# Moving one softmax piece across a block boundary, and re-cutting its batch into pieces of 10, 6, 11 and 11 rows

## The chip, the cores and the metric

The kernel runs on one core of one Trainium2 chip. The metric is device time in microseconds of one execution. The profile is one execution recorded by the hardware profiler, and its span is some 1.7 us shorter than the time of the same run (734.8 us for 736.54).

In the profile's lines, PE is TensorE (matmuls), PEld its weight loads, DVE VectorE, ACT ScalarE, and L536 is line 536 of the kernel. Times in a timeline are microseconds from the span's start.

## The reference

A dynamic convolution, then a feed-forward network with a squared ReLU:

```
w   = softmax(weight_gen over the 7 taps)            # per token and head
out[b, s, h] = sum_k w[b, s, h, k] * x[b, s - 6 + k, h]   # 8 heads of 24 channels
h   = relu(out @ w_in)                                # 192 -> 2048
y   = (h * h) @ w_out                                 # 2048 -> 192
```

There are 8 batches of 4096 tokens. The matmuls of the feed-forward part fill PE; the softmax is side work for ScalarE (exponential) and VectorE (sum, reciprocal, scaling).

## The kernel before

The work is cut into blocks of 1024 tokens (the first two have 512). Each block has 16 units: 6 matmuls into `h`, a ReLU on ScalarE into `t1`, and a square on VectorE into `g`. The output matmuls `M` of block j - 1 are interleaved with the units of block j. A quarter of a block takes two `M` (units 0 to 7, then 8 to 15) of 32 matmuls each, into two banks of PSUM, the memory that the matmuls write. ScalarE then copies one bank into `o_sb`, and VectorE adds the other to it.

```
        nc.scalar.activation(out=t1[:, e], in_=h, func=ActF.Relu)
        n = 2 if PAIRED_FROM <= j and u < NF - 2 else 1    # units 14 and 15: single squares
        if e + 1 >= n:
            a = e + 1 - n
            nc.vector.tensor_tensor(                        # L536
                out=g[:, a : e + 1], in0=t1[:, a : e + 1], in1=t1[:, a : e + 1], op=AluOp.mult
            )
...
    ps_o = ctx.enter_context(tc.tile_pool(name="ps_o", bufs=1, space=...PSUM))   # o0, o1: one buffer each
...
        nc.scalar.copy(out=o_sb, in_=o[0][:, c])            # L574
        if len(o) == 2:
            nc.vector.tensor_tensor(out=o_sb, in0=o[1][:, c], in1=o_sb, op=AluOp.add)   # L576
```

A softmax of a whole batch covers 32 rows per partition and 6 of halo (rows that the next partition holds too). It is cut into four pieces, and each piece is placed at a point (block, unit) of the program: ahead of that unit, after the `M` that precedes it. A piece on VectorE is a sum, a reciprocal, and 4 scalings for each stretch of at most 8 rows that doesn't cross a multiple of 8. Its exponential on ScalarE has a place of its own, some units earlier.

```
        steady_spread = "MuMuuu" * 2 + "MuCMuuu" + "MuMuuu"    # u unit, M output matmuls, C convolution
...
        CUTS = {..., R: (0, 8, 18, 28, R + HALO)}              # default: 8, 10, 10, 10 rows
        CUTS_FOR = {(2, 1): (0, 11, R // 2 + HALO)}
        TIMES = {
            ...
            (3, 0): ((9, 9), (9, 13), (10, 9), (11, 9)),       # the fourth batch
        }
        def soft(s):
            lo, hi = next(s.softs)
            s.total(lo, hi)          # L257
            s.recip(lo, hi)          # L264
            s.scale(lo, hi, nc.vector)   # L272
```

The program orders all instructions by hand, and each engine takes its own in that order. The fourth batch is the first with this four-piece plan, and the only one of them with two pieces in one block: the later batches put one in each of four blocks.

The softmax here doesn't subtract the row's maximum and nothing guards it: scores larger than these inputs give would overflow.

## Time and profile before

| | before |
|---|---|
| time, first 3 runs | 736.59 us median (735.5 to 736.84) |
| profiled span | 734.8 us, clock 1.00 |
| block 9 to 10, first `M` after the convolution to the same place one block on | 23.28 us |
| its neighbours | 22.06, 22.08 us |
| PE idle recorded in that block | 23.28 - 22.60 = 0.68 us |

### The profile page before, as it was taken

The numbers are of one execution on the slowest core, as the hardware profiler recorded it, in microseconds if no ns is written. First come the engines' busy times: TensorE is split into PE (matmuls) and PEld (weight loads), VectorE is DVE, ScalarE is ACT, GpSimd is POOL, SyncE is SP. The second block draws the span as 40 slices with busy tenths as digits, with TensorE's granted clock in tenths as the row PEclk, the third lists the DMA queues.
The fourth block names the chain that finished last, engine by engine and source line by source line (L and its number), as shares of the span: only waits on it lengthen the run. The fifth ranks groups of instructions, "written<-read, shape, count | busy, mean of one in ns | idle before, by whom it ended". The sixth has DMA issues, their size and how long they took to land.

```text
span 734.8 us, 31124 instructions
## 1 busy us (share of the span) xinstructions
PE 725.9 (99%) x14106; PEld 529.4 (72%) x14106; DVE 627.3 (85%) x856; ACT 613.5 (83%) x724; POOL 100.2 (14%) x148
## 2 busy tenths in 40 slices
PE   7999999999999999999999999999999999999998
PEld 3767777777767777777777777777777777777777
DVE  5999898998899988889888889888889888778853
ACT  4998888988888888888888888888888888888883
POOL 7322222320001100011000110010100110001000
PEclk9999999999999999999999999999999999999999
DMA  7846444794444533454433554334544315444012
GB/s 210 130 81 138 80 62 104 144 165 120 92 74 99 122 76 73 66 137 100 80 65 76 116 124 85 59 64 127 103 87 83 61 48 121 66 87 78 29 45 66
DMA packets 126544, 68.71 MB, mean 93 GB/s; under 512 B 85193, under 2 KB 122636, under 8 KB 125900
## 3 DMA queue, kind: packets, MB, share of 16 engines
q1 hardware_dynamic: 80908, 48.12, 22.9%
q0 software_dynamic: 45360, 18.50, 21.6%
q8 instruction: 110, 1.80, 1.0%
q14 instruction: 22, 0.18, 0.1%
q10 hardware_dynamic: 144, 0.10, 0.0%
HBM read 50.18 MB, written 28.70 MB: 107 GB/s over the span
## 4 chain that ended last, share of the span: by engine, by line
PE 70%; DVE 0%; ACT 0%; issue 0%
PE o L560 35%; PE h L518 32%; PE yp L450 3%; DVE g L536 0%; ACT o_sb L574 0%
## 5 line engine op out<-in xcount | busy, mean ns | idle before, releaser
L532 ACT ACTIVATE t<-h 128x1024 f16<-128x1024 f32 x512 | 496.4, 1026 | 60.1 <-PE h L518 59.7
L560 PEld LDWEIGHTS <-g 64*128 64x128 f16 (+1 forms) x8032 | 342.8, 94 | 56.9 <-issue 2.5
L560 PE MATMUL o<-w_o,g 64*128 64x192 f16 (+1 forms) x8032 | 379.7, 243 | 0.7 <-DVE g L536 0.6
L536 DVE TENSOR_TENSOR g<-t 128x2048 f16<-128x2048 f16 (+1 forms) x309 | 309.2, 1037 | 27.6 <-ACT t L532 27.3
L518 PE MATMUL h<-y,w_p 64*128 64x512 f16 x2400 | 291.7, 376 | 0.0
L518 PEld LDWEIGHTS <-w_p 64*128 64x128 f16 x2400 | 113.8, 94 | 94.8
L381 DVE TENSOR_TENSOR bd<-wr,mask 128x4160 f16<-128x4160 f16 (+3 forms) x89 | 149.4, 1703 | 4.7 <-DMA wr<-v_first 4.7
L576 DVE TENSOR_TENSOR o_sb<-o,o_sb 128x384 f32<-128x384 f32 x123 | 68.4, 556 | 62.1 <-ACT o_sb L574 61.3
L333 POOL DMA_DIRECT2D xt<-in_x_dram x62 | 52.1, 844 | 422.6 <-PE yp L450 363.7
L574 ACT COPY o_sb<-o 128x384 f32<-128x384 f32 x129 | 61.5, 477 | 48.0 <-PE o L560 47.5
L518 PE MATMUL h<-y,w_i 64*128 64x512 f16 (+1 forms) x768 | 82.3, 350 | 1.8 <-ACT t L532 0.8
L518 PEld LDWEIGHTS <-w_i 64*128 64x128 f16 x768 | 37.2, 94 | 27.7 <-issue 4.0
L450 PEld LDWEIGHTS <-xt 128*32 128x32 f16 x2000 | 24.4, 95 | 10.6 <-issue 10.6
L272 DVE TENSOR_TENSOR v_big<-ex,rcp 128x112 f16<-128x112 f32 (+5 forms) x180 | 29.9, 237 | 2.1 <-DMA vd<-v_big 1.1
L460 DVE CAST y<-yp 128x1024 f16<-128x1024 f32 x25 | 30.4, 1218 | 0.0
L450 PE MATMUL yp<-bd,xt 128*32 128x104 f16 (+1 forms) x2000 | 28.3, 209 | 0.0
L250 ACT ACTIVATE ex<-wg 128x560 f32<-128x560 f32 (+4 forms) x38 | 25.9, 682 | 1.7 <-DMA wg<-in_weight_gen_dram 1.7
L257 DVE TENSOR_REDUCE ssum<-ex 128x80 f32<-128x560 f32 (+4 forms) x38 | 25.3, 666 | 2.2 <-ACT ex L250 2.2
L460 ACT CAST y<-yp 128x1024 f16<-128x1024 f32 x25 | 25.2, 1007 | 0.0
L264 DVE RECIPROCAL rcp<-ssum 128x80 f32<-128x80 f32 (+4 forms) x38 | 22.8, 600 | 1.3
L323 POOL DMA_DIRECT2D xt<-in_x_dram x7 | 3.9, 555 | 124.7 <-PE yp L450 109.7
L363 POOL DMA_DIRECT2D wr<-v_first x31 | 16.9, 565 | 15.9 <-DVE v_first L272 15.7
(34 smaller groups left out, 95.8 us busy)
## 6 DMA issues: line engine op xcount, KB each, us to landing
out_dram<-o_sb SPq DMA_DIRECT2D x63, 384.0 KB
xt<-in_x_dram POOLq DMA_DIRECT2D x42, 240.0 KB, 5.1
wg<-in_weight_gen_dram SPq DMA_DIRECT2D x4, 1064.0 KB
xt<-in_x_dram POOLq DMA_DIRECT2D x20, 192.0 KB, 4.6
wr<-vd SPq DMA_DIRECT2D x38, 80.0 KB
vd<-v_big SPq DMA_DIRECT2D x5, 512.0 KB
y<-y SPq DMA_DIRECT2D x100, 24.0 KB
wg<-in_weight_gen_dram SPq DMA_DIRECT2D x5, 392.0 KB
```

The lines of the kernel that those rows point to most:

```text
L250: nc.scalar.activation(out=self.ex[:, lo:hi].rearrange("p r g k e -> p (r g) k e"), in_=self.wg[:, lo:hi].rearrange("p r (g e) k -> p (r g ...
L272: eng.tensor_tensor(out=bass.AP(tensor=v.tensor, offset=v.offset + lo * H * SL + lo % SL * 2 + g * SL * 2, ap=[list(v.ap[0]), [H * SL + 2, ...
L333: eng.dma_start(out=dst[:, first:last], in_=ap)
L381: nc.vector.tensor_tensor(out=bd_t[j][:, H * lo : H * (lo + len(tiles) * n)].rearrange("p (g m c) -> p g m c", g=shape[1], c=2 * SL), in0= ...
L450: nc.tensor.matmul(out=yp[p0 : p0 + 32, k - k0, a:b], lhsT=x_t[s][:, i, c0 : c0 + 32], rhs=bd[:, head // 2, e, 0 : b - a], start=True, sto ...
L460: copy(out=y[:, k0 : k0 + 2], in_=yp)
L518: nc.tensor.matmul(out=h[:, half, jj * th : (jj + 1) * th], lhsT=w_in_chunk(w, u * per + jj, slot, half), rhs=y_t[j][r0 : r0 + RT, k, 0:th ...
L532: nc.scalar.activation(out=t1[:, e], in_=h, func=ActF.Relu)
L536: nc.vector.tensor_tensor(out=g[:, a : e + 1], in0=t1[:, a : e + 1], in1=t1[:, a : e + 1], op=AluOp.mult)
L560: nc.tensor.matmul(out=oo[:, cc * Dm : (cc + 1) * Dm], lhsT=g[r0 : r0 + n, cc * P : (cc + 1) * P], rhs=w_o[r0 : r0 + n, fc, :], start=(fc ...
L574: nc.scalar.copy(out=o_sb, in_=o[0][:, c])
L576: nc.vector.tensor_tensor(out=o_sb, in0=o[1][:, c], in1=o_sb, op=AluOp.add)
```

## The change

The intent is to take the second piece out of the way of block 9's last squares and put it where VectorE waits anyway, at the start of block 10, and to make it small enough for that hole. The other pieces take over its rows.

```diff
-        CUTS_FOR = {(2, 1): (0, 11, R // 2 + HALO)}
+        CUTS_FOR = {(2, 1): (0, 11, R // 2 + HALO), (3, 0): (0, 10, 16, 27, R + HALO)}
...
-            (3, 0): ((9, 9), (9, 13), (10, 9), (11, 9)),
+            (3, 0): ((9, 9), (10, 0), (10, 9), (11, 9)),
```

The second piece's exponential stays at the same unit, with 6 rows in place of 10.

## The prediction

> **What bounds the kernel now.** I read the page's busy shares first, then the chain that ended last, then each block by stretches of time, then the instructions in the stretch that stood out.
>
> ```profile
> PE 725.9 (99%) x14106; PEld 529.4 (72%) x14106; DVE 627.3 (85%) x856; ACT 613.5 (83%) x724; POOL 100.2 (14%) x148
> ...
> PE 70%; DVE 0%; ACT 0%; issue 0%
> ```
>
> The first line is busy time per engine, the second the chain's shares. TensorE (PE) is busy for 99% of the span, and the chain followed back from the last instruction is almost all PE. It leaves PE only at 215.71 us, at a VectorE (DVE) square `g`; from there to the end, PE waits for nothing. A microsecond won before that point should therefore come off the end whole, and one not on PE's path is worth nothing.
>
> So I measured PE's period. A two-chunk block runs from the first output matmuls after the convolution to the same place one block on. In the list of stretches (length, busy time and count by engine, granted clock, DMA):
>
> ```profile
> 182.10:204.16 22.06, 22.06 (x437) 16.10 (x434) 19.75 (x28) 18.73 (x24) 2.17 (x3) 1.00 0.43 85
> 204.16:227.44 23.28, 22.60 (x441) 15.96 (x434) 21.45 (x33) 19.33 (x25) 1.71 (x2) 1.00 0.37 69
> 227.44:249.52 22.08, 22.08 (x442) 16.11 (x434) 19.59 (x28) 18.83 (x24) 2.17 (x3) 1.00 0.49 114
> ```
>
> All do the same matmuls at clock 1.00. One lasts 23.28 us where its neighbours last 22.06 and 22.08: 1.20 us are lost there, and DVE has the most work there (21.45 us). PE in order of time, at the end of block 9 and the start of block 10:
>
> ```profile
> 213.98 0.81 PE L518 MATMUL h<-y,w_p 64*128 64x512 f16 x6
> 214.63 0.82 PE L560 MATMUL o<-w_o,g 64*128 64x192 f16 x16
> 215.77 0.94 PE L560 MATMUL o<-w_o,g 64*128 64x192 f16 x12 [0.32 <-DVE g L536]
> 216.97 0.34 PE L560 MATMUL o<-w_o,g 64*128 64x192 f16 x4 [0.26 <-DVE g L536]
> 217.15 2.11 PE L518 MATMUL h<-y,w_p 64*128 64x512 f16 x18
> ```
>
> Elsewhere these 32 output matmuls are one line and occupy 1.32 us from start to next start. Here they are broken twice: the second half-quarter of block 9 uses its units 8 to 15, and `g` of units 12 to 15 is not there. DVE says why:
>
> ```profile
> 211.43 0.56 DVE L576 TENSOR_TENSOR o_sb<-o,o_sb 128x384 f32<-128x384 f32 x1 [0.42 <-ACT o_sb L574]
> 211.90 0.73 DVE L257 TENSOR_REDUCE ssum<-ex 128x80 f32<-128x560 f32 x1
> 212.66 0.65 DVE L264 RECIPROCAL rcp<-ssum 128x80 f32<-128x80 f32 x1
> 213.35 1.23 DVE L272 TENSOR_TENSOR v_big<-ex,rcp 128x112 f16<-128x112 f32 x8
> 214.49 2.43 DVE L536 TENSOR_TENSOR g<-t 128x2048 f16<-128x2048 f16 x3
> 217.85 0.56 DVE L576 TENSOR_TENSOR o_sb<-o,o_sb 128x384 f32<-128x384 f32 x1 [0.94 <-ACT o_sb L574]
> ```
>
> The second softmax piece (10 rows, 211.90 to 214.49: 2.59 us) stands ahead of the block's last three squares, which end only at 216.92. The same place in a block without a second piece:
>
> ```profile
> 278.88 0.56 DVE L576 TENSOR_TENSOR o_sb<-o,o_sb 128x384 f32<-128x384 f32 x1 [0.42 <-ACT o_sb L574]
> 280.08 2.52 DVE L536 TENSOR_TENSOR g<-t 128x2048 f16<-128x2048 f16 x3 [0.64 <-ACT t L532]
> 284.11 0.56 DVE L576 TENSOR_TENSOR o_sb<-o,o_sb 128x384 f32<-128x384 f32 x1 [1.50 <-ACT o_sb L574]
> ```
>
> There the squares begin 1.20 us after the add (before: 3.06 us), and then DVE stands idle for 1.50 us. That hole is where the piece goes.
>
> **What the Trainium skill says.** "Perfetto Trace Analysis", section "Tensor Engine Instruction (MATMUL, LD_WEIGHTS)", states that the ACT and DVE execution queues are strict FIFO; the trace agrees: the squares' inputs were long ready (ScalarE's last ReLU of the block ended at 214.42), yet they started at 214.49, when the piece was through. So position in program order is all that the change alters. The same section says that PE's ends are a model; that bears on the rivals below. "VectorE: DVE Perf Modes", section "Side-by-side: where the cycles go for N=2048 bf16", gives about 1224 ns for a two-source 16-bit operation on 2048 elements; the paired square here takes 1220 ns on average. I use trace durations throughout.
>
> **The change part by part.** No instruction appears or vanishes: the built programs have equal counts on every engine. Pieces of 8, 10, 10, 10 rows become 10, 6, 11, 11. Costs start to start on DVE: 8 rows 1.98 us (206.67 to 208.65), 10 rows 2.59. For 6 and 11 rows, two places of the same kernel:
>
> ```profile
> 123.33 0.49 DVE L257 TENSOR_REDUCE ssum<-ex 128x48 f32<-128x336 f32 x1
> 123.85 0.45 DVE L264 RECIPROCAL rcp<-ssum 128x48 f32<-128x48 f32 x1
> 124.34 0.72 DVE L272 TENSOR_TENSOR v_big<-ex,rcp 128x84 f16<-128x84 f32 x4
> ...
> 184.59 0.78 DVE L257 TENSOR_REDUCE ssum<-ex 128x88 f32<-128x616 f32 x1
> ...
> 189.62 0.55 DVE L576 TENSOR_TENSOR o_sb<-o,o_sb 128x384 f32<-128x384 f32 x1
> ```
>
> Six rows take 1.73 us (to 125.06), eleven 2.75 us (184.59 to 187.34). The DVE sum goes from 1.98 + 3 x 2.59 = 9.75 to 2.59 + 1.73 + 2 x 2.75 = 9.82 us: nothing is saved in work, so all depends on place.
>
> *First piece, 10 rows.* The add after it was at 211.43. The same piece in block 10 starts at 229.95 and its add follows at 234.81, 4.86 later; here 206.67 + 4.86 = 211.53, so 0.10 late. It ends at 212.09; PE's next output matmuls begin at 212.66. No stall.
>
> *Second piece gone from block 9.* As in block 10, the squares start 1.10 after the add: 212.63, and end 2.52 later, 215.15. PE starts the 32 matmuls at 214.63 and needs the last square after 28 of them, 28/32 x 1.32 = 1.15 later, 215.78: 0.63 in hand. The block drops to 22.08: minus 1.20 us.
>
> *Second piece in block 10, 6 rows.* It runs from 215.15 to 216.88. The add behind it would start 1.86 after those matmuls start (284.11 against 282.25), at 216.49; it starts 0.39 late and ends at 217.43. The next output matmuls need the add, as the two PSUM banks have one buffer each; they come after the 32 matmuls (215.95) and three units (1.94), at 217.89. 0.46 in hand. The lateness then shrinks by the idle 0.17 before the next add, whose usual spare is 1.94 - 1.11 = 0.83.
>
> *Third and fourth, 11 rows.* 0.16 later each. The pieces of 11 rows in earlier blocks show the result: the add shown at 189.62 ends at 190.17, PE goes on at 190.58, unbroken.
>
> *ScalarE.* The exponentials stay where they were; 0.63 + 3 x 0.74 = 2.85 us becomes about 0.74 + 0.52 + 2 x 0.79 = 2.84.
>
> Sum: -1.20 + 0 = -1.20 us.
>
> **The rivals.** (a) The moved piece delays the PSUM add until PE waits for it. Against it: 0.46 us in hand. For it: that is little, and a piece of 10 rows there would have overrun by 0.86 - 0.46 = 0.40. If it happens, 0.1 to 0.4 us come back: some 735.7. (b) Only PE's recorded idle time, 0.32 + 0.26 = 0.58, is there to win: 736.0. Against it: the block's length is measured from starts, and modelled ends hide the rest in "busy". (c) The longer first, third or fourth piece makes a stall of its own, 0.1 to 0.3 us: the precedents with 10 and 11 rows in the same slot speak against it. (d) A later wait swallows the gain: no PE wait on another engine is recorded after 217 us, so I give it little.
>
> **Range and chances.** 736.59 - 1.20 = 735.39; the three runs of before have a mean of 736.31, which would give 735.11. I take 735.3. The before runs spread over 1.34 us, as much as the gain, so the range is 734.4 to 736.3. Two per cent is 14.7 us, twelve times the stall: faster by that 0.005, within 0.985, slower 0.01.
>
> **What would show it.** Right: the block is 22.1 us long; the squares run before the 6-row piece; the add after it ends about 0.4 us late with no PE wait; the chain leaves PE earlier than 215 us or not there. Wrong: a PE wait on the `o_sb` add near 218 us, a block over 22.3 us, or a new break at an 11-row piece.

## The result, and the profile after

| | before | after |
|---|---|---|
| time, 6 runs each | 736.25 us median (735.49 to 738.67) | 734.96 us median (734.49 to 735.74) |
| profiled span | 734.8 us | 733.2 us |
| block 9 to 10 | 23.28 us | 22.10 us |

The ratio is 0.998, 95% interval 0.9965 to 0.9996. This ratio and those below are not quite the ratios of the medians (here 0.9982). In the classes used here (2%) the time is the same; the gain of some 1.3 us is small but clear of zero.

The stretches of the kernel after (length, then busy time and count of PE, PEld, DVE, ACT, POOL, then clock and DMA), with the boundary of blocks 9 and 10 in the middle:

```profile
181.56:203.64 22.08, 22.08 (x438) 16.12 (x433) 19.73 (x28) 18.82 (x24) 2.17 (x3) 1.00 0.43 85
203.64:225.74 22.10, 22.10 (x442) 16.10 (x434) 21.12 (x33) 19.29 (x25) 1.72 (x2) 1.00 0.39 72
225.74:247.82 22.08, 22.08 (x439) 16.13 (x432) 19.74 (x28) 18.88 (x24) 2.16 (x3) 1.00 0.48 114
```

The long block is now like its neighbours. VectorE still has most work there (21.12 us), but PE has no gap. The page's chain of work that ended last, shares by engine:

```profile
PE 96%; DVE 1%; DMA 1%; ACT 1%; issue 0%; DVEq 0%
```

Before, the chain stopped at the square that PE had waited for (70% of the span). Now it runs back along PE to the start of the kernel. ("issue" is time in which an engine waited for nothing that the profile shows, DVEq is VectorE's sequencer.) VectorE in order of time at the boundary, kernel after:

```profile
211.01 0.55 DVE L576 TENSOR_TENSOR o_sb<-o,o_sb 128x384 f32<-128x384 f32 x1
212.11 2.52 DVE L536 TENSOR_TENSOR g<-t 128x2048 f16<-128x2048 f16 x3 [0.55 <-ACT t L532]
214.55 0.50 DVE L257 TENSOR_REDUCE ssum<-ex 128x48 f32<-128x336 f32 x1
215.08 0.45 DVE L264 RECIPROCAL rcp<-ssum 128x48 f32<-128x48 f32 x1
215.57 0.72 DVE L272 TENSOR_TENSOR v_big<-ex,rcp 128x84 f16<-128x84 f32 x4
216.20 0.55 DVE L576 TENSOR_TENSOR o_sb<-o,o_sb 128x384 f32<-128x384 f32 x1
```

The squares follow the first add, wait 0.55 us for ScalarE, and end at 214.63; then the piece fills the hole; then comes the next add with no idle before it. PE over the same time:

```profile
214.11 1.48 PE L560 MATMUL o<-w_o,g 64*128 64x192 f16 x32
215.43 2.10 PE L518 MATMUL h<-y,w_p 64*128 64x512 f16 x18
217.38 1.48 PE L560 MATMUL o<-w_o,g 64*128 64x192 f16 x32
```

The 32 output matmuls are one unbroken line again, 1.32 us from start to next start. The add is through at 216.20 + 0.55 = 216.75, and PE takes the banks again at 217.38, so 0.63 us are in hand.

The two spans differ by 1.6 us, more than the block. The same mark, the first `M` of that stretch, lies at 204.16 us in one and 203.64 in the other: 0.52 us of the difference lies ahead of the stretch, and 0.50 of it arose by the first output matmuls of the kernel, which start at 26.50 and 26.00 us. After the stretch, 734.8 - 227.44 = 507.4 us remain before and 733.2 - 225.74 = 507.5 after. So the block gives 1.18 us, and the rest is not the change's.

### The profile page after: what moved, and what is told of

It reads as the page before. It is cut to its first block, busy times and chain, and to the rows that moved or that the text cites. A ratio compares the mean times of both kernels' runs of the same rounds, so it can differ in the third digit from the quotient of the medians.

```text
span 733.2 us, 31124 instructions
## 1 busy us (share of the span) xinstructions
PE 726.3 (99%) x14106; PEld 528.5 (72%) x14106; DVE 627.3 (86%) x856; ACT 613.8 (84%) x724; POOL 100.5 (14%) x148
## 4 chain that ended last, share of the span: by engine, by line
PE 96%; DVE 1%; DMA 1%; ACT 1%; issue 0%; DVEq 0%
PE o L560 47%; PE h L518 45%; PE yp L450 4%; PE yp L487 1%; DVE bd L381 1%; DMA wr<-v_first 1%; ACT t L532 0%; DMA wg<-in_weight_gen_dram 0%; ACT ex L250 0%; DVE v_first L272 0%; ACT y L503 0%; DVE ssum L257 0%; DVE rcp L264 0%; DVE g L536 0%; DVE xt L347 0%
## 5 line engine op out<-in xcount | busy, mean ns | idle before, releaser
L381 DVE TENSOR_TENSOR bd<-wr,mask 128x4160 f16<-128x4160 f16 (+3 forms) x89 | 149.4, 1703 | 4.1 <-DMA wr<-v_first 4.1
```

What stands on the lines that cost most here:

```text
L381: nc.vector.tensor_tensor(out=bd_t[j][:, H * lo : H * (lo + len(tiles) * n)].rearrange("p (g m c) -> p g m c", g=shape[1], c=2 * SL), in0= ...
```

## The experiments

The theory: VectorE takes its queue in order, and at this boundary PE sets it two dates. The last squares must be ready 28 matmuls into the second `M`; the add of `o_sb` must be ready when the next quarter reuses its banks. A piece costs PE whatever it makes either of them late, and nothing else. The rivals: the place alone or the cuts alone do it; any place past the squares is as good; every VectorE microsecond costs; only PE's recorded idle counts.

All eight runs gave the right result. In every profile the measure is the length of the stretch from the first `M` after block 9's convolution to the same place in block 10, undisturbed 22.08 us. Runs 1 to 4 shared nine runs of before (median 735.77 us), runs 5 to 8 seven (736.36 us).

### 1. The place alone (10 rows at the start of block 10)

```diff
-            (3, 0): ((9, 9), (9, 13), (10, 9), (11, 9)),
+            (3, 0): ((9, 9), (10, 0), (10, 9), (11, 9)),
```

> The place alone: pieces 8, 10, 10, 10, the second (10 rows, 2.59 us) moved to the start of block 10. In the kernel after, the 6-row piece (1.73 us) let the add of o_sb end at 216.75, and PE used its bank at 217.38: 0.63 us in hand. My theory (VectorE order against two PE deadlines): 2.59 - 1.73 = 0.86 us later, so PE waits 0.86 - 0.63 = 0.23 us, with some 0.06 of latency 0.2 to 0.3 us: block of 22.3 to 22.4 us (first output matmuls after the convolution to the same place one block on), 735.2 us where the kernel after has 735.0. Rival 'the place alone is the whole cure, the cuts are idle': block 22.08, no PE wait. Rival 'only recorded PE idle time counts': same block length as its recorded idle.

Measured: 735.08 us median of 5, ratio 0.9987 (0.9975 to 1.0). The stretch, and VectorE's and PE's lines at the date:

```profile
204.26:226.70 22.44, 22.31 (x439) 16.88 (x434) 21.07 (x33) 19.44 (x25) 1.72 (x2) 1.00 0.38 71
```

```profile
217.76 0.55 DVE L576 TENSOR_TENSOR o_sb<-o,o_sb 128x384 f32<-128x384 f32 x1
```

```profile
217.99 1.85 PE L560 MATMUL o<-w_o,g 64*128 64x192 f16 x32
```

The add ends at 218.31; PE was due at 217.99, and its 32 matmuls stretch to 1.85 us. The block loses 22.44 - 22.08 = 0.36 us. The expected 0.2 to 0.3 was low because the 6-row piece in the kernel after takes 1.65 us from its start to the next instruction's start, not 1.73: 2.59 - 1.65 - 0.63 = 0.31, and some 0.05 of latency. The place alone wins most of the loss back, but not all. "Only recorded idle counts" falls: PE shows 22.44 - 22.31 = 0.13 us of idle, and no wait on VectorE is listed at all.

### 2. The cuts alone (6 rows, still ahead of the squares)

```diff
-        CUTS_FOR = {(2, 1): (0, 11, R // 2 + HALO)}
+        CUTS_FOR = {(2, 1): (0, 11, R // 2 + HALO), (3, 0): (0, 10, 16, 27, R + HALO)}
```

> The cuts alone: pieces 10, 6, 11, 11, the second left ahead of block 9's last three squares. My theory: the piece is 0.86 us shorter, the squares start at 213.2 and end at 215.64 on the clock of the kernel after; PE resumes the units 0.23 after the last square (as in the kernel before: 216.92 and 217.15), at 215.87 where 215.43 is unbroken: 0.44 us lost, block 22.5 us, so 0.76 of the 1.20 us gained by size alone. Rival 'the place alone matters': block stays 23.2 to 23.3. Rival 'any piece there hurts nothing once it is short': 22.08.

Measured: 735.37 us median of 5, ratio 0.9996 (0.9983 to 1.0008), so the timing doesn't tell it from before. The profile does; PE's lines:

```profile
214.36 1.32 PE L560 MATMUL o<-w_o,g 64*128 64x192 f16 x28
215.86 0.34 PE L560 MATMUL o<-w_o,g 64*128 64x192 f16 x4 [0.18 <-DVE g L536]
```

Only the last 4 matmuls wait, for the square of unit 15, where before also the 12 ahead of them did. The stretch is 203.89 to 226.32, 22.43 us: 0.35 us lost, against 1.20 before. The 0.44 expected was again too much by the 0.09 us of the piece's true length. In the profile either half of the change alone wins about 0.85 us; together they win 1.18.

### 3. Eight rows at the start of block 10

```diff
-... (3, 0): (0, 10, 16, 27, R + HALO)}
+... (3, 0): (0, 8, 16, 27, R + HALO)}
```

(Shown against the kernel after, as in runs 5 to 8.)

> Pieces 8, 8, 11, 11, the second of 8 rows (1.98 us) at the start of block 10. My theory: 0.25 us later than the 6-row piece, 0.63 in hand, so no PE wait: block 22.08 and the time of the kernel after within noise. Rival 'every added VectorE microsecond on that stretch costs': block 22.3.

Measured: 734.92 us median of 5, ratio 0.9985 (0.9971 to 0.9998).

```profile
203.47:225.55 22.08, 22.08 (x441) 16.12 (x434) 20.71 (x29) 19.30 (x25) 1.72 (x2) 1.00 0.39 72
```

No loss: a longer piece in the hole (1.98 us from start to start, for 1.65) is free as long as the add meets its date. Here it ends at 216.91, 0.30 us ahead of PE at 217.21. The stretch as a whole has less VectorE work than in the kernel after (20.71 us for 21.12), so this run alone doesn't refute "every VectorE microsecond costs". Runs 1, 4 and 6 do: with 21.07, 21.09 and 21.11 us of VectorE work in the stretch they lose 0.36, 0 and 0.99 us.

### 4. The kernel after, once more

No edit.

> The kernel after, unchanged, beside the others on this chip: block 22.08, no PE wait on VectorE after 20 us, 0.17% (1.2 us) under before. If the difference to before is outside 0.7 to 1.8 us, the clean part of the earlier comparison is in doubt.

Measured: 734.61 us median of 5, ratio 0.9979 (0.9967 to 0.9992); stretch 203.18 to 225.26, 22.08 us. The medians differ by 1.16 us, as the block does.

### 5. Sixteen rows at the start of block 10

```diff
-... (3, 0): (0, 10, 16, 27, R + HALO)}
+... (3, 0): (0, 8, 24, 31, R + HALO)}
```

> Pieces 8, 16, 7, 7, the 16-row one at the start of block 10. From 2.59 us (10 rows) and 2.75 (11 rows), 0.16 a row: some 3.5 us. In the kernel after, the 6-row piece takes 1.65 us start to start there and leaves 0.63 in hand; my theory: PE waits 3.5 - 1.65 - 0.63 = 1.2 us (1.1 to 1.4), block 23.3, all gain gone, the time that of before. With 6, 8, 10 rows measured at 0, 0, 0.36 us, the loss must rise one for one with the piece beyond the time in hand. Rival 'the start of the block is free for VectorE': 22.1.

Measured: 736.4 us median of 4, ratio 1.0003 (0.9988 to 1.0017). PE's lines:

```profile
217.26 0.24 PE L560 MATMUL o<-w_o,g 64*128 64x192 f16 x1
218.64 1.48 PE L560 MATMUL o<-w_o,g 64*128 64x192 f16 x31 [1.13 <-DVE o_sb L576]
```

The piece took 3.60 us (214.44 to 218.04), the add ended at 218.59. One matmul starts on the bank that ScalarE has already copied; the other bank is not free, and PE waits for the add by name. The stretch is 203.53 to 226.98, 23.45 us: 1.37 lost, the whole gain and a little more. With 6, 8, 10 and 16 rows the losses are 0, 0, 0.36 and 1.37 us: nothing up to the date, then one for one.

### 6. Six rows ahead of the last square only

```diff
-            (3, 0): ((9, 9), (10, 0), (10, 9), (11, 9)),
+            (3, 0): ((9, 9), (9, 15), (10, 9), (11, 9)),
```

> The cuts of after, the 6-row piece between the squares of units 14 and 15 of block 9. My theory: the pair and unit 14 are squared in time, the piece runs 213.85 to 215.50 on the clock of the kernel after, the last square ends at 216.17, PE goes on 0.23 later at 216.40 where 215.43 is unbroken: 0.97 us lost (0.9 to 1.1), block 23.05: worse than ahead of all three squares (0.35 measured), where DVE's idle 0.55 us before them takes up part of the piece. Rival 'fewer squares stand behind it, so it costs less than ahead of all three': under 0.35, block under 22.4.

Measured: 735.98 us median of 4, ratio 0.9994 (0.9979 to 1.0009).

```profile
216.24 0.34 PE L560 MATMUL o<-w_o,g 64*128 64x192 f16 x4 [0.82 <-DVE g L536]
```

The stretch is 203.63 to 226.70, 23.07 us: 0.99 us lost, as worked out (0.97), and nearly three times as much as ahead of all three squares. Fewer squares stand behind the piece, but the last square's date is what counts, and the 0.55 us in which VectorE waits for ScalarE lie ahead of the pair and no longer take up part of the piece. The kernel derives the place of an exponential from that of its piece, so here it moves too, from unit 12 to unit 8 of block 9. That isn't the cause: the ReLUs that feed these squares end 0.21 us before the second `M` starts (213.89 and 214.10), in the kernel after 0.20 (213.91 and 214.11).

### 7. Six rows behind the add

```diff
-            (3, 0): ((9, 9), (10, 0), (10, 9), (11, 9)),
+            (3, 0): ((9, 9), (10, 1), (10, 9), (11, 9)),
```

> The cuts of after, the 6-row piece one unit later: behind the add of o_sb, ahead of the band. My theory: it now fills no hole; the band and two pairs of squares follow without idle, so the next add ends 223.1 to 223.2 on the clock of the kernel after, where PE needs it at 222.60: 0.5 to 0.6 us lost, block 22.6 to 22.7. Rival 'anywhere past the squares is as good': 22.08.

Measured: 735.92 us median of 5, ratio 0.9991 (0.9974 to 1.0007). One of the five, the profiled one, took 741.25 us (the ratio of the plain means with it would be 1.0005); its trace has a wait of 3.50 us at the start of the kernel (`h` on a ReLU), long before the change. The stretch itself is 209.07 to 232.10, 23.03 us: 0.95 lost. PE's lines:

```profile
228.03 0.24 PE L560 MATMUL o<-w_o,g 64*128 64x192 f16 x1
228.80 1.48 PE L560 MATMUL o<-w_o,g 64*128 64x192 f16 x31 [0.53 <-DVE o_sb L576]
```

The direction was right, the size not: 0.5 to 0.6 was expected. 0.77 us are lost at the next add (228.03 to 228.80). I had set the add ahead of the piece 0.15 us too early (see the next section), and 0.05 is latency. The other 0.18 is lost at the convolution behind it: it starts at 230.86, but the second band that it needs (`bd`, the softmax weights laid out as a matrix for it, L381) is ready only at 230.99, and it occupies 1.24 us where 1.06 to 1.08 is usual. That the band is the cause is inferred from these times; no wait is recorded. "Anywhere past the squares is as good" falls: one unit later, the piece pushes a full queue, and its dates are the next add and, it seems, the convolution, which the theory had not listed. The exponential moves here too, to the start of block 10, but ScalarE's copy before the first add keeps its 1.52 us behind the `M` (221.06 and 219.54; in the kernel after 215.63 and 214.11).

### 8. Sixteen rows as the third piece

```diff
-... (3, 0): (0, 10, 16, 27, R + HALO)}
+... (3, 0): (0, 10, 16, 32, R + HALO)}
```

> Pieces 10, 6, 16, 6: block 9 and the second piece as in after, the third with 16 rows in place of 11 in block 10. In the kernel after the add behind the 11-row piece ends at 233.83 and PE needs it at 234.24: 0.41 in hand. My theory: a piece of 3.5 us comes 0.75 later, so the block from 225.74 on is 0.3 to 0.4 us longer than 22.08, perhaps 0.1 more from the squares behind it; block 9 to 10 stays 22.08. Rival 'the slot after the convolution has room for any size': 22.08 in both.

Measured: 735.38 us median of 4, ratio 0.9986 (0.9971 to 1.0001). The first stretch is 204.57 to 226.65, 22.08 us; the next, with the 16-row piece after the convolution, is 226.65 to 249.21, 22.56 us: 0.48 lost.

```profile
235.62 1.48 PE L560 MATMUL o<-w_o,g 64*128 64x192 f16 x31 [0.23 <-DVE o_sb L576]
```

The add ended at 235.57, and PE was due at 235.15. So that slot has a date too, and the 11 rows of the change are on the safe side of it. No run here is better than the kernel after: no PE wait on another engine remains in its profile past the first 25 us.

## Why the prediction was right or wrong

**The bound, and the loss of 1.20 us.** Right. The block went from 23.28 to 22.10 us, the median from 736.25 to 734.96, inside the range. The estimate of 735.3 was 0.34 above the median; three more runs of before lowered its median by 0.34 as well.

**First piece, 10 rows, 0.10 late.** Right. In the kernel after its add starts 2.13 us after the preceding 32 matmuls start (211.01 - 208.88), against 2.03 before (211.43 - 209.40). No stall.

**Second piece gone from block 9.** Right. The squares start 1.10 after the add and end 0.52 after the second `M` starts (214.63 - 214.11), as predicted. (The prediction's 214.42 is the end of the last of three ReLUs. The first of them, which the pair of squares needs, started at 211.57; in the kernel after the squares start 1.05 after it, 211.06 to 212.11. So by some 212.62 the pair could have begun, and it did wait for the piece.)

**Second piece in block 10: add 0.39 late, 0.46 in hand.** The mechanism was right, both sizes were off. Measured, the add starts 2.09 us after the 32 matmuls (216.20 - 214.11). Its undisturbed delay is 2.02, so it was only 0.07 late, and 0.63 us were in hand. Two terms were mis-sized. The delay "1.86" was taken as 284.11 from the timeline minus 282.25 from the chain of waits; the two views set the start of such matmuls about 0.16 us apart (217.15 and 217.31 for the same units before), so the true delay is 2.02. And a piece was reckoned to the end of its last scaling and placed after the end of the last square, though the next VectorE instruction starts 0.08 before that end: 1.65 us in place of 1.73, from 0.08 earlier. ("Perfetto Trace Analysis", section "DVE / Act Engine Instruction (TENSOR_ADD, Activation, etc)", has the recorded window end at the write's acknowledgement, after the next instruction may begin its prefetch. The traces agree: consecutive VectorE records overlap, here by 0.08 us.) 0.16 + 0.08 + 0.08 = 0.32 is the difference between 0.39 and 0.07. Only the latter two touch the time in hand, which went from 0.46 to 0.63. The "usual spare" of 0.83 at the next add has the 0.16 in it as well: it is 0.67 (221.93 to 222.60).

**Third and fourth piece, 11 rows.** Right. The adds end at 233.83 and 255.92, as in the precedent 0.41 us ahead of PE for the former (234.24). Run 8 shows where this would have ended.

**The rivals.** (a), a stall at the add, did not happen; run 1 shows it for 10 rows, 0.36 us where the prediction said 0.40. That these agree so well is partly luck: the prediction had 0.86 - 0.46, measured are 0.94 - 0.63 and 0.05 of latency. (b), only the recorded idle is to be won, fell: the block's gain is 1.18 us, twice 0.58, and run 1 loses 0.36 us with 0.13 recorded. The lines of the weight loads, which the prediction didn't use, come nearer. `g` is what PE loads as weights in an `M`, and in the kernel before the loads wait for it three times:

```profile
215.76 0.28 PEld L560 LDWEIGHTS <-g 64*128 64x128 f16 x8 [0.54 <-DVE g L536]
216.37 0.12 PEld L560 LDWEIGHTS <-g 64*128 64x128 f16 x4 [0.32 <-DVE g L536]
216.97 0.11 PEld L560 LDWEIGHTS <-g 64*128 64x128 f16 x4 [0.49 <-DVE g L536]
```

That is 1.35 us for a loss of 1.20; in run 2 it is 0.40 for 0.35, in run 6 1.04 for 0.99, and in run 1 a gap of 0.49, put down to no engine, for 0.36. (c) and (d) did not happen: the neighbouring stretches are 22.08 us, and the time remaining after the stretch is 507.4 and 507.5 us.

**What stays open.** The medians can't resolve less than half a microsecond: the ratio of run 2 (0.9996) and that of run 1 (0.9987) belong to the same loss in the profile. The order of the experiments rests on the profiles, one execution each. The start of the kernel varies by as much as the gain, and the runs don't show why: in nine of the ten profiles the first output matmuls start between 25.01 and 26.50 us and the mark at block 9's convolution lies between 203.18 and 204.57; in the tenth, run 7's, there is the wait of 3.50 us.

## What to carry to other kernels

When one engine is the bound and runs a repeating pattern, compare the length of each repeat from start to start rather than its busy share; a single long repeat shows where to look. On an in-order helper engine, list the dates that the bounding engine sets, and place side work in the hole between the last thing that has a date and the next thing that can't start yet, cut to the hole's size. Measure such margins from starts in one view alone.

## What the Trainium skill lacked or had wrong

- "Perfetto Trace Analysis", section "Tensor Engine Instruction (MATMUL, LD_WEIGHTS)", says that PE's ends are estimated, but not how much of a wait that hides. Here 1.20 us of lost time showed as 0.68 us of idle before, and 0.36 us as 0.13 in run 1, with no wait of the matmuls listed there. The gaps of the weight loads were 1.35 and 0.49 us.
- No page has this: after a wait on a PSUM bank, PE's output groups are recorded longer until the next convolution (1.54 in place of 1.48 us in runs 1, 5 and 8), and the weight loads' busy time in the stretch rises from 16.10 in the kernel after to 16.88 us in run 1. The cause is open.
